# Second batch of an attention kernel: the middle heads' q and k turned by DMA transfers, the first heads' on TensorE behind the last first-layer products

## The chip, the cores and the metric

The kernel runs on one core of one Trainium2 chip. The metric is the device time in microseconds of one execution. Five engines work from queues of their own, each in order: TensorE (PE; its weight loads are listed apart as PEld), VectorE (DVE), ScalarE (ACT), GpSimd (POOL) and SyncE (SP), which here does little but issue DMA transfers. Sixteen DMA engines move the data; in the profile, queue q1 holds what SP issues, q0 what POOL issues.

## The reference, cut to what matters

Eight batches of twelve heads, 448 tokens, 64 columns each; then a two-layer network over the 3584 tokens with 768 columns, 2048 hidden:

```python
q_n, k_n = (rmsnorm(q, g_q), rmsnorm(k, g_k))
scores = scale * np.matmul(q_n, k_n.transpose(0, 1, 3, 2))
attn = softmax(scores)                       # over the keys
x = (attn @ v) -> tokens x (heads * columns)
h = x @ w_in
g = 0.5 * h * (1 + tanh(c * (h + 0.044715 * h**3)))
out = g @ w_out
```

(`softmax` and the arrow stand for the reference's longer lines.)

## The kernel before, in words

The twelve heads of a batch are worked as three groups of four, c = 0, 1, 2: the first, middle and last heads. A group is seven tiles of 64 tokens (t = 0 to 6). For every batch b:

- q and k are loaded by SP (`load`), squared, summed (`total`, L173), and normed (`normed`, L278) into bf16 tiles `nrmq` and `nrmk`, tokens on the partitions.
- They are turned so that the head columns lie on the partitions, into `qT` and `kT`, in one of two ways. `trans` turns on PE: seven transposes for q and seven for k into PSUM (`turn`, L296), each evicted by one instruction (`put`): k always by DVE, which multiplies it with the gains of both norms on the way (L305), q by ACT (L307) or DVE (L309). `transposed` turns by two DMA transposes that SP issues (`dma_trans`, L319), one for q and one for k, straight into `qT` and `kT`; the gains are then multiplied into `kT` in place by DVE (`gain`, L325).
- `unit` (L335) makes the scores of one tile of one group on PE, four products into one PSUM tile pair; `exp` (L343) takes the exponential on ACT. `add_exps` (L355 to L362) sums the exponentials over tiles on DVE, so that PE's sums (`products` with what = 0) need fewer products; `products` with what = 1 gives attn @ v (L387). `turned`, `recip`, `spread` (L397, L402, L409) make the reciprocal of the sums on DVE, and `quad_x` (L422) multiplies it in and writes `xT`.
- The first layer (`mm1_pair`, L556, in batch 0; `mm1_turn`, L537, in batch 1) multiplies `xT` with `win` and puts the GELU into `g` on ACT. The second layer (`quartered`, L495) multiplies `g` with `wout`. It runs interleaved with the attention of the next batch.

That interleaving is an order written out by hand. `SECOND` is the one for b = 1. In its first string, `u` is a unit of scores (the numbering is c = 0, t = 0 to 6, then c = 1, and so on), `8r` are eight rounds of the second layer (four products each), `s` and `x` are the sums and attn @ v of the next group. Its second string is the order of DVE's work: `A0` is the first sum of exponentials of group 0 (L355), `E0` the eviction of a finished second-layer tile (L518), `B0`, `F0`, `G0` the further sums. `L0`, `K0` and the like are hooks: the list `extra` says what is put there, and `first` what DVE gets before the first unit.

Before that, batch 0's first layer runs as f = 0 to 7; after step f the functions that the list `m1` has for f are called. From f = 3 on a step is one pair of products over six weight tiles each, with its GELU (`mm1_pair`). At step 0, DVE and POOL norm the first and last heads of batch 1; at step 2, DVE norms the middle heads (`normed_both(1, 1, nc.vector)`). At step 6 the first heads are turned on PE with q evicted by ACT; at step 7, behind the last pair, the middle heads are turned on PE and evicted by DVE. Under `first`, DVE issues two one-element writes that let SP's loads for batch 2 go (`late_loads`), and then the weight sums `in_sums` (L587 to L589, two groups of three instructions). The last heads of batch 1 are turned by transfers, let go by DVE at `L0` (`late_transposed`), and get their gains at `K0`.

The PSUM tile pairs go round in one list (`rounds`): a unit takes the oldest, and the second layer takes the oldest when its first round is issued.

Of the kernel before, what the change touches and what calls it, by code (L numbers as in the profile page):

```python
# [17 lines left out]
def kernel(  # L18
# [11 lines left out]
    nc = tc.nc  # L30
    B, H, S, D = q.shape
# [86 lines left out]
    def load(b, c, n, parts=1, engs=(nc.sync,)):  # L118
        t = rawqk.tile([P, 2, NT, D], F32, tag=f"raw{n}", name=f"raw{n}")
        src = {"q": q, "k": k}[n]  # L120
        raws[n, b, c] = t
        m = 2 // parts
        return [
            lambda i=i: engs[i].dma_start(
                t[:, i * m:(i + 1) * m].rearrange("p a t d -> p a (t d)"),
                src[b, 4 * c + 2 * i * m:4 * c + 2 * (i + 1) * m].rearrange(
                    "(a r) (p t) d -> (r p) a (t d)", r=2, t=NT
                ),
            )
            for i in range(parts)  # L130
        ]
# [6 lines left out]
    def late_loads(b, c):  # L138

        for n in "qk":  # L140
            for go in load(b, c, n):
                nc.vector.memset(raws[n, b, c][:1, 0, 0, :1], 0.0)
                go()
# [99 lines left out]
    def rsqrt_last(b, c=slice(NCH - 1, NCH)):  # L243

        flat, m = "p c n a t -> p (c n a t)", (c.stop - c.start) * 4 * NT
        y, ms = rinvs[b][:, c].rearrange(flat), sss[b][:, c].rearrange(flat)
        dst, z, u = y, None, ms
        if not steady():
            z, u = oall[0][:, S:S + m], oall[0][:, S + m:S + 2 * m]
            dst = place(b, 1)  # L250
        t = smp.tile([P, NCH * 4 * NT], F32, tag="lg", name="lg")[:, :m]
        nc.vector.tensor_scalar(u, ms, 1.0 / D, 1e-6, op0=ALU.mult, op1=ALU.add)
        nc.vector.tensor_scalar(
            y.bitcast(I32), u.bitcast(I32), -0.5, float(0x5F3759DF), op0=ALU.mult, op1=ALU.add
        )
        for i in range(3):
            if z is not None:
                nc.vector.tensor_copy(z, y)
            half = t if z is None else z
            nc.vector.tensor_mul(t, y if z is None else z, y)  # L260
            nc.vector.scalar_tensor_tensor(half, t, -0.5, u, op0=ALU.mult, op1=ALU.mult)
            nc.vector.scalar_tensor_tensor(
                y if i < 2 else dst, half, 1.5, y, op0=ALU.add, op1=ALU.mult
            )
# [8 lines left out]
    def normed(b, c, n, eng, ts=slice(0, NT)):  # L273
        if (n, b, c) not in nrms:
            nrms[n, b, c] = nrmp.tile([P, NT, 2, D], BF16, tag=f"nrm{n}", name=f"nrm{n}")
        m = ts.stop - ts.start
        root = rinvs[b][:, seat(b, c), "qk".index(n)] if eng is nc.gpsimd else roots[n, b, c]
        eng.tensor_mul(  # L278
            nrms[n, b, c][:, ts].rearrange("p t a d -> p a t d"),
            raws[n, b, c][:, :, ts],  # L280
            root[:, :, ts].to_broadcast([P, 2, m, D]),
        )

    def qT_of(b):
        if b not in qT:
            qT[b] = qkp.tile([128, NCH, NT, 2, R], BF16, tag="qT", name="qT")
        return qT[b]
# [3 lines left out]
    def turn(b, c, n, ts=slice(0, NT)):  # L291

        if ts.start == 0 and ts.stop == NT:
            tps[n] = ps_m.tile([128, 1024], BF16, tag="mm", name="tp")
        for t in range(ts.start, ts.stop):
            nc.tensor.transpose(  # L296
                tps[n][:, t * 128:(t + 1) * 128],
                nrms[n, b, c][:, t].rearrange("p a d -> p (a d)"), ident,
            )

    def put(b, c, n, ts=slice(0, NT), eng=nc.vector):
        dst = (kT if n == "k" else qT_of(b))[:, c, ts]
        src = tps[n][:, :TR].rearrange("p (t r s) -> p t r s", r=2, s=R)[:, ts]
        if n == "k":
            nc.vector.tensor_scalar(dst, src, gcol[:, 0:1], None, op0=ALU.mult)  # L305
        elif eng is nc.scalar:
            nc.scalar.copy(dst, src)  # L307
        else:
            nc.vector.tensor_copy(dst, src)  # L309

    def trans(b, c, eng=nc.vector):
        for n in "qk":
            turn(b, c, n)
            put(b, c, n, eng=eng)

    def dma_trans(b, c, n):

        dst = kT[:, c] if n == "k" else qT_of(b)[:, c]
        nc.sync.dma_start_transpose(  # L319
            dst.rearrange("p t r s -> p t (r s)"),  # L320
            nrms[n, b, c].rearrange("p t a d -> p (t a d)"),
        )

    def gain(b, c):
        nc.vector.tensor_scalar(kT[:, c], kT[:, c], gcol[:, 0:1], None, op0=ALU.mult)  # L325
# [252 lines left out]
    def blocks_of(half, grp):  # L578
        lo, hi = (half * nf // 2 + n for n in BLOCKS[grp])
        return slice(lo * 128, hi * 128)  # L580

    def in_sums(grp):

        f1, f2 = blocks_of(0, grp), blocks_of(1, grp)
        a11, a21, a12, a22 = wv[:, 0, :, f1], wv[:, 0, :, f2], wv[:, 1, :, f1], wv[:, 1, :, f2]
        s2, s3, s4 = wxs[grp]
        nc.vector.tensor_sub(s3, a21, a11)  # L587
        nc.vector.tensor_add(s2, s3, a22)
        nc.vector.tensor_sub(s4, a12, s2)  # L589
# [6 lines left out]
    class Seven:  # L596
# [254 lines left out]
    )  # L851
    SECOND = (
# [441 lines left out]
    def transposed(b, c):  # L1294
        for n in "qk":
            dma_trans(b, c, n)

    def late_transposed(b, c):

        for n in "qk":  # L1300
            dst = kT if n == "k" else qT_of(b)
            nc.vector.memset(dst[:1, c, 0, 0, :1], 0.0)
        transposed(b, c)
# [11 lines left out]
    def normed_both(b, c, eng):  # L1315
        for n in "qk":
            normed(b, c, n, eng)

    for b in range(B):
        m1, side, extra, ends = [], [], [], []  # L1320
        if b == 0:
# [4 lines left out]
                   lambda: normed(1, 0, "k", nc.gpsimd)),  # L1326
                  (2, lambda: total(1, 1, "q"), lambda: total(1, 1, "k"),
                   lambda: normed(1, 0, "q", nc.vector), lambda: rsqrt_last(1),
                   lambda: normed_both(1, 1, nc.vector)),
                  (6, lambda: trans(1, 0, nc.scalar)),  # L1330
                  (7, lambda: trans(1, 1))]
            extra += [("first", lambda: late_loads(2, 0)), ("first", lambda: in_sums("A")), ("first", lambda: in_sums("H")), ("L0", lambda: late_transposed(1, 2)),
                      ("L0", lambda: late_loads(2, 1)), ("a0", lambda: late_loads(2, 2)),
                      ("K0", lambda: gain(1, 2))]

# [147 lines left out]
```

## Time and profile before

| what | value |
|---|---|
| time, median of 3 runs | 381.84 us (381.73 to 381.91) |
| the profiled execution's own time | 381.82 us |
| its span, first to last instruction | 380.0 us |
| PE busy | 371.4 us, 98% |
| DVE busy | 306.3 us, 81% |
| ACT busy | 296.8 us, 78% |
| POOL busy | 140.0 us, 37% |
| mean granted TensorE clock | 0.998 |

The stretch of the change lies between about 46 and 76 us of the span. "Busy" counts instructions, not waits, and an engine with a high share over the whole span need not be the one that sets the pace in a stretch; the chain of waits, followed back from the last instruction, says which it was. A transfer's landing is counted from its issue on the queue.

### The profile page before, as it was taken

What the parts mean: (1) busy time and instruction counts of PE and PEld (TensorE: products, weight loads), DVE (VectorE), ACT (ScalarE), POOL (GpSimd) and SP (SyncE); (2) the same over time, 40 slices, a digit from 0 to 9 for tenths busy, and PEclk for the clock granted to TensorE, in tenths of its full rate; (3) what the DMA queues carried; (4) which work ended last, traced back from release to release, by engine and by line L of the source; (5) the groups of instructions that cost most, each with busy time, mean ns of one, the idle gap of its engine ahead of it and who ended that gap; (6) DMA issues with size and microseconds to landing.
All of it is one profiled execution on the core that took longest, in us unless ns stands there. A gap on an engine that the chain in (4) does not pass through costs nothing.

```text
span 380.0 us, 14862 instructions
## 1 busy us (share of the span) xinstructions
PE 371.4 (98%) x6634; PEld 285.5 (75%) x6634; DVE 306.3 (81%) x469; ACT 296.8 (78%) x383; POOL 140.0 (37%) x127
## 2 busy tenths in 40 slices
PE   8899999999999999999999999999999999999995
PEld 5565577777888977879678876779678786789863
DVE  4999989996899678994799767995699848899863
ACT  6995589767997799976997889977998679966700
POOL 5997503358102780048500781038700560000000
PEclk9999999999999999999999999999999999999999
DMA  7999998799822896258942798139563393320033
GB/s 250 324 240 210 210 245 206 236 160 238 192 54 66 197 242 116 46 115 209 232 104 47 179 203 192 45 86 199 128 111 80 78 121 58 80 57 11 2 73 96
DMA packets 64597, 54.52 MB, mean 143 GB/s; under 512 B 37652, under 2 KB 60436, under 8 KB 64532
## 3 DMA queue, kind: packets, MB, share of 16 engines
q1 hardware_dynamic: 54016, 41.04, 44.2%
q0 software_dynamic: 10128, 11.80, 19.1%
q8 instruction: 52, 0.85, 1.0%
q10 hardware_dynamic: 388, 0.72, 0.5%
q14 instruction: 13, 0.11, 0.1%
HBM read 45.61 MB, written 11.01 MB: 149 GB/s over the span
## 4 chain that ended last, share of the span: by engine, by line
PE 86%; ACT 6%; DVE 4%; DMA 1%; issue 1%; POOL 0%; DVEq 0%
PE t L495 31%; PE t L665 20%; PE t L335 7%; PE t L387 7%; ACT ex L343 5%; PE t L1058 5%; PE t L537 5%; PE t L556 4%; PE t L704 3%; PE t L717 3%; DMA rawq<-in_q_dram 1%; DVE st L397 1%; DVE xT L422 1%; PE h L436 1%; DVE rb L409 1%
## 5 line engine op out<-in xcount | busy, mean ns | idle before, releaser
L343 ACT ACTIVATE ex<-t,shift 128x896 bf16<-128x896 f32 x168 | 157.1, 1012 | 4.2 <-PE t L335 3.4
L495 PE MATMUL t<-wout,g 64*64 64x384 bf16 (+1 forms) x3456 | 150.0, 305 | 0.0
L495 PEld LDWEIGHTS <-g 64*64 64x64 bf16 x3456 | 103.5, 107 | 29.3 <-issue 2.0
L335 PE MATMUL t<-qT,kT 64*64 64x448 bf16 x672 | 57.0, 351 | 1.4 <-ACT ex L343 0.6
L173 DVE TENSOR_REDUCE ss<-sq 128x14 f32<-128x896 f32 (+3 forms) x50 | 44.4, 911 | 9.9 <-ACT sq L162 5.2
L1186 POOL COPY mark<-es 1x1 bf16<-1x1 bf16 x7 | 1.2, 177 | 127.6 <-DVE es L362 118.5
L665 PEld LDWEIGHTS <-win 128*128 128x128 bf16 x456 | 43.7, 98 | 3.5 <-issue 2.1
L278 POOL TENSOR_TENSOR nrmq<-rawq,rinv 128x896 bf16<-128x896 f32 (+1 forms) x21 | 34.8, 1659 | 19.0 <-ACT rinv L205 10.7
L278 POOL TENSOR_TENSOR nrmk<-rawk,rinv 128x896 bf16<-128x896 f32 (+1 forms) x21 | 34.4, 1640 | 0.0
L387 PE MATMUL t<-ex,vb 64*64 64x448 bf16 x588 | 31.9, 350 | 0.0
L335 PEld LDWEIGHTS <-kT 64*64 64x64 bf16 x672 | 23.4, 106 | 9.3 <-DVE kT L305 1.2
L387 PEld LDWEIGHTS <-vb 64*64 64x64 bf16 x672 | 23.3, 107 | 7.5 <-issue 0.9
L689 ACT ACTIVATE g<-t 128x896 bf16<-128x896 f32 (+1 forms) x36 | 26.1, 758 | 3.6 <-DVE t L683 3.6
L397 DVE STREAM_TRANSPOSE st<-t 128x448 f32<-128x448 f32 x42 | 24.8, 628 | 5.0 <-PE t L387 2.9
L355 DVE TENSOR_TENSOR es<-ex 128x1792 bf16<-128x1792 bf16 x21 | 22.3, 1063 | 7.5 <-ACT ex L343 7.5
L409 DVE STREAM_TRANSPOSE rb<-rc 128x896 f32<-128x896 f32 (+1 forms) x25 | 26.7, 1067 | 0.3
L665 PE MATMUL t<-xs,win 128*128 128x224 bf16 x228 | 24.9, 259 | 0.0
L665 PE MATMUL t<-xT,win 128*128 128x224 bf16 x228 | 24.6, 259 | 0.3
L513 ACT COPY osb<-t 128x768 f32<-128x768 f32 (+1 forms) x18 | 12.6, 702 | 14.0 <-PE t L495 14.0
L422 DVE TENSOR_TENSOR xT<-t,rb 128x896 bf16<-128x896 f32 x21 | 22.8, 1086 | 0.9
L164 POOL TENSOR_TENSOR sq<-rawk 128x896 f32<-128x896 f32 (+1 forms) x14 | 21.9, 1569 | 1.1 <-DMA rawk<-in_k_dram 1.1
L358 DVE TENSOR_TENSOR es<-es,ex 128x1792 bf16<-128x1792 bf16 x21 | 22.3, 1063 | 0.0
(167 smaller groups left out, 574.9 us busy)
## 6 DMA issues: line engine op xcount, KB each, us to landing
rawq<-in_q_dram SPq DMA_DIRECT2D x22, 448.0 KB, 4.4
rawk<-in_k_dram SPq DMA_DIRECT2D x22, 448.0 KB, 5.4
out_dram<-osb SPq DMA_DIRECT2D x38, 192.0 KB, 2.9
vb<-in_v_dram POOLq DMA_DIRECT2D x6, 672.0 KB, 7.2
win<-in_moe_w_in_dram POOLq DMA_DIRECT2D x8, 384.0 KB, 11.4
out_dram<-osb SPq DMA_DIRECT2D x31, 96.0 KB, 2.6
wout<-in_moe_w_out_dram POOLq DMA_DIRECT2D x3, 768.0 KB, 17.8
vb<-in_v_dram POOLq DMA_DIRECT2D x2, 448.0 KB, 15.8
```

What stands on the lines that cost most here:

```text
L173: nc.vector.reduce_sum(sss[b][:, seat(b, c), "qk".index(n), hs, ts], squares(b, c, n, hs, ts), axis=AX.X)
L278: eng.tensor_mul(nrms[n, b, c][:, ts].rearrange("p t a d -> p a t d"), raws[n, b, c][:, :, ts], root[:, :, ts].to_broadcast([P, 2, m, D]),)
L335: nc.tensor.matmul(sc[r * R:(r + 1) * R, a, :S], kT[rs, c, t, r], qT[b][rs, c, :, r], start=True, stop=True,)
L343: nc.scalar.activation(exs[b, c][:, t], scs.pop((b, c, t))[:, :, :S], AF.Exp, scale=scale, bias=shift)
L355: nc.vector.tensor_add(es, ex[:, :2], ex[:, 2:4])
L387: nc.tensor.matmul(o[r][a * D:(a + 1) * D], vb[min(b, 1)][rs, 2 * c + a, i] if what else ones[rs], es[i][rs, a], start=(i == 0), stop=(i = ...
L397: nc.vector.transpose(st[:, r].rearrange("p a b -> p (a b)"), o[r])
L409: nc.vector.transpose(oas["rb"][:, rs].rearrange("p r s -> p (r s)"), rc.to_broadcast([128, (rs.stop - rs.start) * m, 32]),)
L422: nc.vector.tensor_mul(xT[b][:, 2 * c:2 * c + 2], oas["o", c, 1][:, :, :S], oas["rb"])
L495: mm = nc.tensor.matmul(o[a * R:(a + 1) * R, bank, :hi - lo], g[rs, f, at:at + R], wout[rs, f, lo:hi], start=(n == 0), stop=(n == len(step ...
L665: nc.tensor.matmul(t[:, bank, n * QS:(n + 1) * QS], lhs[:, m, n * 128:(n + 1) * 128], self.rhs[i][:, m], start=i == owner and n == m == 0, ...
L689: nc.scalar.activation(g[:, f:f + m, lo:lo + QS], (self.of(name) if src is None else src).rearrange("p r (n s) -> p r n s", n=2), AF.Gelu_ ...
```

## The change

For batch 1 only. The middle heads (c = 1) are no longer turned on PE: at step 2, straight after they are normed, SP issues the two DMA transposes, and their gains are multiplied in place by DVE at the end of the work under `first`. The first heads (c = 0) are turned on PE at step 7 and no longer at step 6, and q is evicted by DVE and no longer by ACT. The written order begins with six rounds of the second layer, then the first unit, then three rounds, where it began with the first unit and eight rounds; up to the fourth unit the number of rounds is the same as before (17).

```diff
     SECOND = (
-        "u 8r uu 9r u 7r uu 10r u 3r u 5r u 2r u 4r us 6r u 3r u 1r u 6r xu 4r u 5r u 1r u"
+        "6r u 3r uu 8r u 7r uu 10r u 3r u 5r u 2r u 4r us 6r u 3r u 1r u 6r xu 4r u 5r u 1r u"
         " 3r s 1r u 2r u 10r u 2r x 1r s 3r x",
...
                    lambda: normed(1, 0, "q", nc.vector), lambda: rsqrt_last(1),
-                   lambda: normed_both(1, 1, nc.vector)),
-                  (6, lambda: trans(1, 0, nc.scalar)),
-                  (7, lambda: trans(1, 1))]
-            extra += [("first", lambda: late_loads(2, 0)), ("first", lambda: in_sums("A")), ("first", lambda: in_sums("H")), ("L0", lambda: late_transposed(1, 2)),
+                   lambda: normed_both(1, 1, nc.vector), lambda: transposed(1, 1)),
+                  (7, lambda: trans(1, 0))]
+            extra += [("first", lambda: late_loads(2, 0)), ("first", lambda: in_sums("A")), ("first", lambda: in_sums("H")), ("first", lambda: gain(1, 1)), ("L0", lambda: late_transposed(1, 2)),
                       ("L0", lambda: late_loads(2, 1)), ("a0", lambda: late_loads(2, 2)),
                       ("K0", lambda: gain(1, 2))]
```

VectorE's queue from the end of the norming of the middle heads to the first work at `L0`, before (`tp` is a PSUM tile of turned q or k, `wx` and `vb_121` the homes of the weight sums, `es` a sum of exponentials):

```order
L305 TENSOR_SCALAR kT<-tp,gcols 128x896
L309 COPY qT<-tp 128x896
L305 TENSOR_SCALAR kT<-tp,gcols 128x896
L142 MEMSET rawq 1x1
L142 MEMSET rawk 1x1
L587 TENSOR_TENSOR wx<-win 128x1536
L588 TENSOR_TENSOR wx<-wx,win 128x1536
L589 TENSOR_TENSOR wx<-win,wx 128x1536
L587 TENSOR_TENSOR vb_121<-win 128x768
L588 TENSOR_TENSOR vb_121<-vb_121,win 128x768
L589 TENSOR_TENSOR vb_121<-win,vb_121 128x768
L355 TENSOR_TENSOR es<-ex 128x1792
```

and now:

```order
L309 COPY qT<-tp 128x896
L305 TENSOR_SCALAR kT<-tp,gcols 128x896
L142 MEMSET rawq 1x1
L142 MEMSET rawk 1x1
L587 TENSOR_TENSOR wx<-win 128x1536
L588 TENSOR_TENSOR wx<-wx,win 128x1536
L589 TENSOR_TENSOR wx<-win,wx 128x1536
L587 TENSOR_TENSOR vb_121<-win 128x768
L588 TENSOR_TENSOR vb_121<-vb_121,win 128x768
L589 TENSOR_TENSOR vb_121<-win,vb_121 128x768
L325 TENSOR_SCALAR kT<-kT,gcols 128x896
L355 TENSOR_TENSOR es<-ex 128x1792
```

Of three evictions two are left, now both of the first heads, and the gains of the middle heads (L325) stand between the weight sums and the first sum of exponentials.

SP's queue of DMA issues at the same place, as a difference; the two loads behind the new rows are those of batch 2 that DVE lets go under `first`:

```order
 L124 DMA rawq<-in_q_dram 128x2x448
 L124 DMA rawk<-in_k_dram 128x2x448
+L319 DMA_TRANSPOSE qT<-nrmq 128x7x128
+L319 DMA_TRANSPOSE kT<-nrmk 128x7x128
 L124 DMA rawq<-in_q_dram 128x2x448
 L124 DMA rawk<-in_k_dram 128x2x448
```

The two new transposes go out ahead of those loads; nothing else on this queue has moved.

## The prediction

> **What bounds the kernel now.** I read the page first, then the chain of waits around the place that the change touches, then VectorE's timeline there, then the DMA queues in stretches.
>
> ```profile
> span 380.0 us, 14862 instructions
> PE 86%; ACT 6%; DVE 4%; DMA 1%; issue 1%; POOL 0%; DVEq 0%
> ```
>
> TensorE (PE) sets the end nearly everywhere, so a microsecond taken from its queue is worth one if nothing else is late. The profiled execution took 381.82 us, 1.82 more than its span; the median is 381.84, so sums against either agree. In the chain of waits (start, length, what) the stretch from the last products of the first layer to those of the second batch reads:
>
> ```profile
> 47.39 2.27 PE t L556 x12
> 49.66 0.78 PE tp L296 x14
> 50.44 0.31 PE t L335 x4
> ...
> 54.19 1.14 PE t L495 x28
> ...
> 57.52 0.49 PE t L495 x12
> 58.01 0.19 PE t L335 x4
> ...
> 67.49 3.71 ACT ex L343 x4
> ...
> 71.25 1.08 DVE es L358
> ...
> 75.30 1.19 DVE st L397 x2
> ...
> 76.53 3.56 PE t L537 x69
> ```
>
> Fourteen transposes (0.78) stand on PE's path before the first scores. PE holds the path to 67.5, ScalarE's (ACT) exponentials to 71.2, VectorE (DVE) to 76.5, and then PE's first-layer products wait for DVE's last reading of a PSUM tile. Three engines are therefore close together here. DVE's timeline (start, length, line, what, wait before it):
>
> ```profile
> 47.28 1.08 DVE L278 TENSOR_TENSOR nrmk<-rawk,o 128x896 bf16<-128x896 f32 x1
> 48.27 0.68 DVE L305 TENSOR_SCALAR kT<-tp,gcols 128x896 bf16<-128x896 bf16 x1
> 50.09 0.62 DVE L309 COPY qT<-tp 128x896 bf16<-128x896 bf16 x1 [1.14 <-PE tp L296]
> 50.63 0.68 DVE L305 TENSOR_SCALAR kT<-tp,gcols 128x896 bf16<-128x896 bf16 x1
> 51.24 0.95 DVE L587 TENSOR_TENSOR wx<-win 128x1536 bf16<-128x1536 bf16 x1
> ...
> 55.74 1.08 DVE L355 TENSOR_TENSOR es<-ex 128x1792 bf16<-128x1792 bf16 x1
> ...
> 57.05 1.02 DVE L518 COPY osb<-t 128x384 f32<-128x384 f32 x2 [0.17 <-PE t L495]
> ...
> 61.03 1.18 DVE L397 STREAM_TRANSPOSE st<-t 128x448 f32<-128x448 f32 x2 [0.56 <-PE t L387]
> ...
> 64.54 0.40 DVE L325 TENSOR_SCALAR kT<-kT,gcols 128x896 bf16<-128x896 bf16 x1
> ```
>
> From 51.24 DVE runs without a gap into L355, the first sum of exponentials. After 55.74 it waits twice, 0.17 and 0.56; the 0.56 is the way from its own last sum (L362) through PE's sums back to L397, so it moves with DVE and is no reserve. The table by stretches (PE, weight loads, DVE, ACT, POOL) shows what follows:
>
> ```profile
> 61.00:76.50 15.50, 15.40 (x352) 11.11 (x345) 15.18 (x24) 13.26 (x19) 6.37 (x7) 1.00 0.79 238
> ```
>
> DVE is busy 15.18 of 15.50 us. What it is late at 61 it is late at 76.5, and PE behind it.
>
> **The change part by part.** *Removed from PE:* the 14 transposes of the middle heads, 0.78 us. Those of the first heads move behind the last pair of products, 14 as before. *ACT* loses one eviction ahead of its last GELU, where it waited for PE anyway.
>
> ```profile
> 50.63 1.28 ACT L1438 ACT_TABLE_LOAD   x1
> 51.92 13.00 ACT L343 ACTIVATE ex<-t,shift 128x896 bf16<-128x896 f32 x14
> ```
>
> The last products end 0.78 earlier, and so do the GELU, the table load, and the first exponential (51.92 to 51.14). The transposes of the first heads then run from 48.9 to 49.7; DVE evicts q and k by its two rows above, 0.78 earlier: 49.31 and 49.85 to 50.53. Six rounds of second-layer products (24 products; 28 took 1.14, so 0.98) lead PE to 50.6 before the first scores, which therefore wait for nothing. That exposed wait I cost at 0; without the six rounds it would be about 0.9. The rounds are only moved. On DVE one eviction from PSUM (0.68) becomes one scaling in SBUF (L325, 0.40), and the weight sums begin at 50.5 and end at 55.05.
>
> *Added:* two DMA transposes and a wait. SP issues them as soon as DVE has made q (47.4) and k (48.4); its queue is empty then. The wait is DVE's L325 for k's landing. Queued behind it on DVE is L355 and everything above after 55.05; behind that on PE are the scores of the middle heads (the L335 piece at 58.01 is their first), and the sums that feed L397. So the change hangs on when k lands. DMA issues on SP (start, length), and landings (us after issue, last number) of the loads and transposes nearest in time, asked for by the stretch of their issue:
>
> ```profile
> 51.39 0.37 SPq L124 DMA_DIRECT2D rawq<-in_q_dram  x1
> ...
> 57.02 1.33 SPq L319 DMA_TRANSPOSE qT<-nrmq  x1
> 58.46 1.24 SPq L319 DMA_TRANSPOSE kT<-nrmk  x1
> ```
>
> ```profile
> rawq<-in_q_dram SPq DMA_DIRECT2D x1, 448.0 KB, 6.6
> qT<-nrmq SPq DMA_TRANSPOSE x1, 3.4
> kT<-nrmk SPq DMA_TRANSPOSE x1, 3.0
> vb<-in_v_dram POOLq DMA_DIRECT2D x1, 448.0 KB, 21.5
> ```
>
> By the 3.0 of 58.46 k would land at 52 and be hidden under the weight sums. But these transposes ran when the engines were free. Packets by queue (packets, MB, share) of four stretches, 52.7 to 54, 50.5 to 58, 55 to 58, and 58.2 to 60.9:
>
> ```profile
> q0 software_dynamic: 298, 0.27, 125.5%
> ```
>
> ```profile
> q0 software_dynamic: 948, 0.89, 72.2%
> ```
>
> ```profile
> q0 software_dynamic: 60, 0.05, 10.1%
> ```
>
> ```profile
> q1 hardware_dynamic: 1870, 0.49, 101.6%
> ```
>
> POOL's queue q0 (the second layer's weights, then v) fills all 16 engines until about 55. From 52.7 to 54 SP's queue q1 moves nothing at all, though a load was issued on it at 51.39; that load lands at 51.39 + 6.6 = 57.99. Earlier, from 22 to 25.5, with both queues full, they went one packet for one:
>
> ```profile
> q0 software_dynamic: 248, 0.47, 71.2%
> q1 hardware_dynamic: 247, 0.44, 38.0%
> ```
>
> The two transposes are some 1,800 small packets (1,870 in the 2.7 us in which both ran, a few of a load among them). Whether q1 waits for q0 or alternates with it, the 948 packets of q0 give out before the second transpose does, so k ends behind q0. *Earliest*: q0's bulk ends at 55.0, q has shared until then, k alone takes 1.35 (half of 2.7), and landing lags by 0.6 (61.46 against 60.9): 57.0. *Latest*: one engine carries q0 to the last (60 packets after 55; the v load issued at 36.95 lands at 58.45), all of both follows: 58.45 + 2.7 = 61.1. *Taken*: the transposes stand on q1 ahead of the load that landed at 57.99, so q gets its place, and k comes 1.0 later (60.42 to 61.46 is the spacing of the two that ran free): 59.0. Then L325 to 59.4, and L355 starts at 59.4 instead of 55.74: +3.66, of which the 0.17 wait is absorbed: **+3.5**. PE's 0.78 and ACT's 0.78 are lost in it, because both then wait for DVE. The stalled middle scores alone would cost less (59.4 against 58.0). Sum: 381.82 + 3.5 = **385.3**; with 57.0 and 61.1 it is 383.3 and 387.4.
>
> [...] The row 58.2 to 60.9 shows 0.49 MB in 2.7 us, about 180 GB/s, with a load among it; the measurement decides. [...]
>
> **The rivals.** *Hidden after all* (not slower): k lands by 55.05. For it: the weight sums cover 4.6 us, and the free transposes took 3.0. Against it: no q1 packet in 52.7 to 54. L325 then ends at 55.45, L355 gains 0.29, the 0.17 goes: 381.82 − 0.46 = 381.4. Only if DVE's full stretch gives way too does PE's whole 0.78 come through: 381.0. From a landing 0.5 us later, at 55.5, it is a loss.
>
> *Long turns*: SP's transposes pass in long bursts between q0's packets, and it is the weights that come late. POOL's last weight load and the landings of the last two:
>
> ```profile
> 33.44 0.73 POOL L1176 DMA_DIRECT2D wout<-in_moe_w_out_dram  x1
> ...
> wout<-in_moe_w_out_dram POOLq DMA_DIRECT2D x2, 384.0 KB, 19.5
> ```
>
> The last lands near 53.4 (a median of two: the first, issued 0.7 earlier, lands a little sooner); PE needs it in the piece at 54.19, about 54.8, after the change 54.0. Pushed back by all of 2.7 us it comes at 56.1, PE stands 2.1, and 381.82 − 0.78 + 2.1 = 383.1, with k in time. Against it: one for one at 22 to 25.5. [...]
>
> That the transfers don't start early, so that the change doesn't do what it says, gets no chance of its own: nothing unfinished stands ahead of them on SP, whose next issue before was at 51.39.
>
> **How the numbers follow.** Forecast 0.72, spanning 383.3 to 387.4; long turns 0.06; hidden 0.16; hidden with PE's gain whole 0.05; later still than 61.1, 0.01. No change is within 0.2% (0.76 us), about what a measurement here can tell: faster 0.05 (381.0), same 0.16 (381.4), slower 0.79. The range reaches to the hidden case, 381.3 to 387.0; the likeliest case's own is 383.3 to 387.0.
>
> **What would show it.** Right: DVE's L325 after the weight sums waits 2 to 6 us on a DMA; the first transpose lands near 58, the second near 59; L355 starts near 59.4; PE's middle scores wait for kT; PE's first L537 comes near 79. The head start shows too: first exponential near 51.1. Wrong: L325 starts at once at 55; or the stall at L325 is there and DVE makes it up before L537; or PE waits for the weights near 54.

## The result, and the profile after

The changed kernel takes 386.80 us (median of 6 executions, 385.57 to 388.67) against 381.94 for the kernel before (6, 381.73 to 383.64): a ratio of 1.0129, 95% interval 1.0108 to 1.0149. It is slower by some 4.9 us; its profiled execution took 385.96, with a span of 384.2 (before: 381.82 and 380.0). Medians are of all executions; the ratios leave out those more than 1.5% above the fastest of the same kernel, which are two of ten for no_wait and one of ten for k_alone.

The chain of waits of the changed kernel, from the end of the first layer to the second batch's products (start, length, what):

```profile
37.45 11.17 PE t L556 x60
48.63 10.44 DMA kT<-nrmk
...
59.46 1.08 DVE es L355
...
79.54 1.19 DVE st L397 x2
...
80.77 3.37 PE t L537 x65
```

The DMA that turns k now stands on the path, with 10.44 us from issue to landing. On the path the products of L537 begin at 80.77 instead of 76.53. VectorE's timeline shows the wait in its place:

```profile
49.77 0.68 DVE L305 TENSOR_SCALAR kT<-tp,gcols 128x896 bf16<-128x896 bf16 x1
...
54.41 0.56 DVE L589 TENSOR_TENSOR vb<-win,vb 128x768 bf16<-128x768 bf16 x1
59.09 0.45 DVE L325 TENSOR_SCALAR kT<-kT,gcols 128x896 bf16<-128x896 bf16 x1 [4.12 <-DMA kT<-nrmk]
59.46 1.08 DVE L355 TENSOR_TENSOR es<-ex 128x1792 bf16<-128x1792 bf16 x1
...
63.32 0.62 DVE L362 TENSOR_TENSOR es<-es,ex 128x896 bf16<-128x896 bf16 x1
65.26 1.18 DVE L397 STREAM_TRANSPOSE st<-t 128x448 f32<-128x448 f32 x2 [1.31 <-PE t L387]
```

The weight sums end at 54.97, and VectorE then stands 4.12 us for k. L397 waits 1.31 where it waited 0.56 before. The two new issues on SP's queue:

```profile
47.19 1.33 SPq L319 DMA_TRANSPOSE qT<-nrmq  x1
48.63 4.50 SPq L319 DMA_TRANSPOSE kT<-nrmk  x1
53.23 0.52 SPq L124 DMA_DIRECT2D rawq<-in_q_dram  x1
```

The second issue holds SP for 4.50 us, so the load behind it leaves at 53.23 instead of 51.39. From 47 to 51, with the first transpose issued at 47.19, POOL's queue q0 moves 582 packets and q1 none at all; q1's first packet comes 3.9 us behind that issue, between 51.05 and 51.10. From then on they share: from 54.0 to 54.5 the two queues move (packets, MB, share):

```profile
q0 software_dynamic: 84, 0.07, 89.4%
q1 hardware_dynamic: 84, 0.02, 32.2%
```

Over this stretch they get one packet for one. A transposed packet here carries 0.25 KB (0.02 MB in 84), a packet of q0 about 0.8 KB, so the transposes get few of the bytes that move. The late first packet and the sharing together made a landing of 10.44 us out of one of 3.0; how much each of them took was not separated.

TensorE's middle scores wait for the gain, and one piece later again:

```profile
59.60 0.38 PE L335 MATMUL t<-qT,kT 64*64 64x448 bf16 x4 [2.27 <-DVE kT L325]
...
61.61 0.59 PE L335 MATMUL t<-qT,kT 64*64 64x448 bf16 x4 [0.82 <-DVE osb L518]
...
64.61 0.53 PE L387 MATMUL t<-es,ones 64*64 64x448 bf16 x4
```

TensorE then gets a lower clock. The table by stretches (stretch, its length, then PE, weight loads, VectorE, ScalarE and POOL, each with its count; the three last numbers are granted clock, DMA share, GB/s):

```profile
60.00:62.00 2.00, 1.18 (x28) 0.68 (x24) 2.00 (x8) 1.01 (x1) 0.00 (x0) 0.87 0.49 163
62.00:64.00 2.00, 2.00 (x32) 1.40 (x28) 1.81 (x3) 1.75 (x2) 0.00 (x0) 0.50 1.16 186
64.00:66.00 2.00, 2.00 (x44) 1.49 (x40) 0.74 (x2) 1.27 (x2) 1.99 (x3) 0.77 0.81 127
```

From 62 to 64 TensorE is busy throughout at half the clock and makes 32 products; from 66 to 68, at 1.00, it makes 56. VectorE's last sum (L362) ends at 63.94, but TensorE's queue comes to the sums' products (the L387 piece) only at 64.61. This is why L397 waits longer than before.

### The profile page after: what moved, and what is told of

Read it like the earlier page. It is cut to its first block, busy times and chain, and to the rows that moved or that the text cites. A ratio compares the mean times of both kernels' runs of the same rounds, so it can differ in the third digit from the quotient of the medians.

```text
span 384.2 us, 14839 instructions
## 1 busy us (share of the span) xinstructions
PE 371.4 (97%) x6620; PEld 284.7 (74%) x6620; DVE 305.6 (80%) x469; ACT 296.9 (77%) x382; POOL 140.2 (36%) x127
## 3 DMA queue, kind: packets, MB, share of 16 engines
q1 hardware_dynamic: 55872, 41.50, 44.6%
## 4 chain that ended last, share of the span: by engine, by line
PE 83%; ACT 6%; DVE 5%; DMA 4%; issue 1%; POOL 0%; DVEq 0%
PE t L495 29%; PE t L665 20%; PE t L387 7%; PE t L335 7%; ACT ex L343 5%; PE t L1058 5%; PE t L537 5%; PE t L556 4%; PE t L704 3%; PE t L717 3%; DMA kT<-nrmk 3%; DMA rawq<-in_q_dram 1%; DVE st L397 1%; DVE xT L422 1%; PE h L436 1%
## 5 line engine op out<-in xcount | busy, mean ns | idle before, releaser
L495 PE MATMUL t<-wout,g 64*64 64x384 bf16 (+1 forms) x3456 | 152.3, 306 | 0.1
L335 PE MATMUL t<-qT,kT 64*64 64x448 bf16 x672 | 58.7, 355 | 4.5 <-DVE kT L325 2.3
L335 PEld LDWEIGHTS <-kT 64*64 64x64 bf16 x672 | 24.2, 107 | 13.2 <-DVE kT L325 2.6
L387 PE MATMUL t<-ex,vb 64*64 64x448 bf16 x588 | 32.0, 350 | 0.0
L397 DVE STREAM_TRANSPOSE st<-t 128x448 f32<-128x448 f32 x42 | 24.8, 629 | 6.1 <-PE t L387 4.0
L387 PEld LDWEIGHTS <-vb 64*64 64x64 bf16 x672 | 23.7, 107 | 7.3 <-issue 1.0
L355 DVE TENSOR_TENSOR es<-ex 128x1792 bf16<-128x1792 bf16 x21 | 22.3, 1061 | 7.1 <-ACT ex L343 7.1
```

Source lines behind the costliest of these rows:

```text
L335: nc.tensor.matmul(sc[r * R:(r + 1) * R, a, :S], kT[rs, c, t, r], qT[b][rs, c, :, r], start=True, stop=True,)
L355: nc.vector.tensor_add(es, ex[:, :2], ex[:, 2:4])
L387: nc.tensor.matmul(o[r][a * D:(a + 1) * D], vb[min(b, 1)][rs, 2 * c + a, i] if what else ones[rs], es[i][rs, a], start=(i == 0), stop=(i = ...
L397: nc.vector.transpose(st[:, r].rearrange("p a b -> p (a b)"), o[r])
L495: mm = nc.tensor.matmul(o[a * R:(a + 1) * R, bank, :hi - lo], g[rs, f, at:at + R], wout[rs, f, lo:hi], start=(n == 0), stop=(n == len(step ...
```

## The experiments

Thirteen timelines are compared by one ruler. VectorE makes 24 reciprocals (L402, one for each of the 8 batches' 3 groups). For each kernel the start of such an instruction less its start in the kernel before (20.19, 62.24, 71.02, 120.78, 150.20, 340.33 us) says how late the program is there; the same difference at the first one, which lies ahead of anything changed and is between −0.24 and +1.15, is taken off. L402 and its neighbours move by one or two lines where a kernel has lines added.

| kernel | batch 1, first (62.24) | batch 1, second (71.02) | batch 2, third (120.78) | batch 3, first (150.20) | last (340.33) | median time, us |
|---|---|---|---|---|---|---|
| the change | 4.32 | 4.31 | 4.32 | 4.69 | 4.69 | 386.80 |
| again | 4.03 | 4.02 | 4.13 | 4.82 | 4.77 | 386.17 (one) |
| v_after_gain | 0.41 | 3.67 | 3.69 | 3.69 | 4.18 | 386.19 |
| v_after_sums | 1.45 | 1.44 | 1.77 | 2.72 | 3.02 | 383.30 |
| before_v_after_sums | 0.29 | 0.29 | 0.29 | 0.30 | 0.33 | 381.92 |
| gain_late | 3.95 | 3.97 | 4.02 | 4.40 | 4.37 | 386.27 |
| fillers | 4.15 | 4.15 | 4.15 | 4.15 | 4.16 | 385.78 |
| both_late | 0.18 | 1.09 | 1.07 | 1.07 | 1.08 | 384.13 |
| no_wait | −0.61 | 2.17 | 2.16 | 2.16 | 2.17 | 384.37 |
| nw_again | −0.60 | 1.68 | 2.09 | 2.72 | 3.30 | 384.65 (one) |
| k_alone | −0.61 | 0.54 | 0.53 | 0.53 | 1.11 | 382.62 |
| no_transfers | −0.61 | −0.61 | −0.61 | 0.08 | 2.03 | 383.27 |
| nt_again | −0.61 | −0.61 | −0.60 | 0.06 | 0.04 | 381.78 (one) |

The first column's reciprocal serves the first heads; its sums are made while the middle heads are scored. The kernel before gave medians of 381.9 to 382.1 in every comparison.

### The change once more

The changed kernel, unaltered, for a second trace.

> The changed kernel a second time, unaltered, for a second profile: its six times lie 3 us apart (385.6 to 388.7), and the one profile cannot say where. Theory: k's transpose lands behind POOL's queue at 57 to 61 us, VectorE's L325 waits for it, PE stands idle and then gets about half the clock for some microseconds; a later landing or a longer half clock gives the longer times. Expected: L325 starts 58 to 61, first L397 of the stretch 64.5 to 68, and all of the difference to the first profile lies before the first products of batch 1's first layer (L537, 80.8 there). Rival: the spread arises later in the program, and L537 starts at 80.8 again whatever the time is.

It took 386.17 us. VectorE:

```profile
59.66 0.45 DVE L325 TENSOR_SCALAR kT<-kT,gcols 128x896 bf16<-128x896 bf16 x1 [4.59 <-DMA kT<-nrmk]
...
65.09 1.18 DVE L397 STREAM_TRANSPOSE st<-t 128x448 f32<-128x448 f32 x2 [0.57 <-PE t L387]
```

The wait comes back at 4.59 us. The clock fell here too (0.64 from 60 to 62, 0.51 from 62 to 64), and yet L397 waits 0.57 as before: k was 0.57 later, and the sums were no later. So the fall of the clock need not cost anything. The expectation that all of the difference to the first profile lies ahead of L537 missed: at the second reciprocal this trace is 0.29 less late than the first profile, and from batch 3 on 0.1 later.

### What k shares the engines with: v moved behind k

In the changed kernel POOL issues batch 1's v in two loads near 37 us, behind the weights. Here it issues v in one load when the middle heads' gain is done.

```diff
-  ..., lambda: load_v(1, 0, 2), lambda: load_v(1, 2, 4)),
...
   ("first", lambda: gain(1, 1)),
+  ("first", lambda: gpsimd_waits(kT[:1, 1, 0, 0, :1])), ("first", lambda: load_v(1, 0, HP)),
```

> Batch 1's v is loaded in one transfer that POOL issues only when the middle heads' gains are multiplied in, so that POOL's queue holds nothing but the second layer's weights when the transposes go. Theory (k waits its turn behind and among POOL's packets): k lands by 54.5 to 55.5, L325 follows the weight sums at once or within 0.5 us, no stretch of PE below 0.9 of the clock, time 381.4 (381.0 to 381.9). Rival (the transposes are slow by themselves when issued at 47, since the second one held SP for 4.5 us): k still lands at 57 or later and the time stays above 383.5. If v then comes too late for attn @ v (63 us), PE waits there instead and the time is 383 to 385 although L325 doesn't wait.

It took 386.19 us (385.86 to 388.63), ratio 1.0126 (1.0092 to 1.0159). VectorE's two gains of the batch, the middle heads' and the last heads':

```profile
56.13 0.45 DVE L325 TENSOR_SCALAR kT<-kT,gcols 128x896 bf16<-128x896 bf16 x1 [0.97 <-DMA kT<-nrmk]
...
68.33 0.45 DVE L325 TENSOR_SCALAR kT<-kT,gcols 128x896 bf16<-128x896 bf16 x1 [3.19 <-DMA kT<-nrmk]
```

The middle k lands 3 us sooner, the wait shrinks from 4.12 to 0.97, and the batch is only 0.41 late there. It still lands 7.3 us after its issue, and later than the 54.5 to 55.5 expected. But v, issued at 57.57, now runs against the last heads' transposes (issued 57.68 and 59.53), and their gain, which waited for nothing before, waits 3.19. TensorE first waits 1.53 for v itself, up to 66.14, as the expectation's last sentence had it, and then 1.19 for that gain, up to 68.84. The crowd has moved one group on and costs nearly the same.

### v between the two, and the same in the kernel before

v goes after the first weight sum (issued 53.60).

```diff
   ("first", lambda: in_sums("A")),
+  ("first", lambda: gpsimd_waits(wx[:1, 2, 0, :1])), ("first", lambda: load_v(1, 0, HP)),
   ("first", lambda: in_sums("H")),
```

> As the kernel before in this call, but v is let go earlier, when the first group of VectorE's weight sums is done (about 53.3 us), so that it lands with time to spare. Theory: as there, 381.4 (381.0 to 381.9), v lands by 61. Rival (transposes slow by themselves): above 383.5. A third way: v's packets at 55 still meet the second transpose, k lands near 56, and the time is 382.3.

> The kernel before with only this later load of v (when the first group of weight sums is done): the control, which separates what the later load does by itself from what it does for the transposes. Theory: nothing waits for v before 63 us, so 381.8 as before (381.5 to 382.1). Rival: the late load of v is a gain or a loss of its own of over 0.5 us, by what it frees or crowds among the loads of batch 2.

With the change 383.30 us (381.95 to 384.57), ratio 1.0030 (1.0010 to 1.0051); in the kernel before 381.92, ratio 1.0003 (0.9993 to 1.0014). So v's place alone costs nothing, and v in front of k is worth 3 us to the change (4.32 against 1.45 at the first reciprocal). The time lies 1 us above the third way's 382.3 and under the rival's 383.5; 381.4 was missed. What is left, VectorE and then TensorE:

```profile
56.81 0.45 DVE L325 TENSOR_SCALAR kT<-kT,gcols 128x896 bf16<-128x896 bf16 x1 [2.01 <-DMA kT<-nrmk]
```

```profile
55.30 0.52 PE L495 MATMUL t<-wout,g 64*64 64x384 bf16 x8 [1.14 <-DMA wout<-in_moe_w_out_dram]
```

VectorE still waits 2.01 for k, although POOL's queue moves only 49 packets from 52 to 55; what holds k there was not found. And now TensorE waits 1.14 for the weights. From 50 to 52 this kernel's queues moved

```profile
q1 hardware_dynamic: 372, 0.10, 104.7%
q0 software_dynamic: 175, 0.25, 68.2%
```

two packets of the transposes for one of the weights. The one for one of the changed kernel is no rule, and the wait that the rival with the late weights describes is there in this kernel.

### Which queue pays for the wait: the gain moved behind the sums

```diff
-  ("first", lambda: gain(1, 1)),
+  ("J0", lambda: gain(1, 1)),
```

> The changed kernel with the middle heads' gain moved on VectorE's queue from ahead of the first sum of exponentials to behind the last one (L362) of the first heads. Theory, VectorE's queue behind the wait is what the wait costs: the first sum of exponentials starts near 55.1 instead of 59.46, VectorE gets to the gain near 59.5 to 60 and k has landed by then (59.1), TensorE's middle scores start near 60.2, VectorE's L397 comes near 63.5 instead of 65.3, and the time is about 384.3 us (383.5 to 385.2). Rival, TensorE's standing still ahead of the middle scores sets the cost by itself: then the time stays within 0.5 us of the changed kernel's 386.2 to 386.8. The fall of the clock after TensorE's stand stays in both.

386.27 us (385.91 to 386.96), ratio 1.0095 (1.0065 to 1.0126): the rival's number, and the expected 384.3 fell. VectorE now does its five sums and evictions first, and the gain without a wait:

```profile
60.92 0.45 DVE L325 TENSOR_SCALAR kT<-kT,gcols 128x896 bf16<-128x896 bf16 x1
66.12 1.18 DVE L397 STREAM_TRANSPOSE st<-t 128x448 f32<-128x448 f32 x2 [4.76 <-PE t L387]
```

(This trace runs 1.15 later from the start.) TensorE:

```profile
61.42 0.38 PE L335 MATMUL t<-qT,kT 64*64 64x448 bf16 x4 [2.88 <-DVE kT L325]
```

VectorE is free from 61.4 and waits 4.76 us for TensorE, whose first middle scores start at 61.42 and whose sums for L397 stand behind four pieces of middle scores, three of them at a lower clock (0.63 from 62 to 64, 0.52 from 64 to 66). So VectorE's queue is not the only one that carries the delay: TensorE's order alone does it. The clock falls here after a single stand of 2.88 us.

### The clock: work for TensorE during the wait

```diff
 def unit(b, c, t):
+    if (b, c, t) == (1, 1, 0):
+        idle(12, sc[:, 0])
```

(the tile is the unit's own, which its scores then overwrite).

> The changed kernel with twelve products of a constant tile put ahead of the middle heads' first scores on TensorE's queue (about 2.2 us of work whose result nobody reads), so that TensorE works during most of the wait for k. Theory, the clock of one half after the stand is what made the delay 4.2 and not 3.5 us: k still lands near 59 and the gain runs then, but the granted clock stays at 1.00 between 61 and 65, the middle scores take 0.39 us apiece, VectorE's first L397 waits 0.56 instead of 1.31, and the time is 0.7 us under the changed kernel's (385.5 against 386.2 for a like run). Rival, the clock falls for another reason or the later pieces do not matter: no difference over 0.3 us, or the clock still falls.

385.78 us (385.44 to 387.26), ratio 1.0088 (1.0053 to 1.0122). VectorE, and the stretch in which the changed kernel had half the clock:

```profile
59.73 0.45 DVE L325 TENSOR_SCALAR kT<-kT,gcols 128x896 bf16<-128x896 bf16 x1 [4.71 <-DMA kT<-nrmk]
...
65.15 1.18 DVE L399 STREAM_TRANSPOSE st<-t 128x448 f32<-128x448 f32 x2 [0.56 <-PE t L389]
```

```profile
62.00:64.00 2.00, 1.74 (x36) 1.15 (x35) 1.86 (x4) 1.32 (x2) 0.00 (x0) 1.00 0.87 141
```

The clock stays at 1.00 and L397 waits 0.56, as the theory had it. The stand ahead of the middle scores is down to 0.44; the later one of 0.82 is still there. That the fall came from TensorE standing is shown; that it costs 0.7 us is not, since "again" had both the fall and the short wait, and the intervals of the two kernels overlap.

### Both cures together

v after the first weight sum, and the gain behind the first sum of exponentials (hook `L0`).

> The kernel that lets v go late (after the first weight sum) and has the middle heads' gain behind the first sum of exponentials instead of ahead of it. Theory: k lands at 56.4 as in the kernel with the late v alone, the first sum of exponentials starts near 55.1 and covers the wait but for 0.7 us, the first L397 comes at 61.6 to 61.9 (62.23 with the late v alone, 61.03 before), and the 1.1 us that TensorE waits for wout stays: 382.3 to 383.0 us, not under the kernel before. Rival, VectorE's wait was all that was left of the loss: 381.4 us or less, faster than before.

384.13 us (381.73 to 385.54), ratio 1.0045 (1.0020 to 1.0070); the profiled execution took 382.81.

```profile
56.52 0.45 DVE L325 TENSOR_SCALAR kT<-kT,gcols 128x896 bf16<-128x896 bf16 x1 [0.54 <-DMA kT<-nrmk]
...
61.15 1.18 DVE L397 STREAM_TRANSPOSE st<-t 128x448 f32<-128x448 f32 x2 [0.56 <-PE t L387]
```

The wait for the middle k is down to 0.54 and the batch 0.18 late, better than the 0.6 to 0.9 expected. The last heads are 1.09 late all the same, and the time is not under that of the kernel before; the median is even above the 383.0 that was expected at most, and the one trace, of a shorter execution, does not show why. The rival, in which VectorE's wait was all that was left, fell.

### Nobody waits for k

```diff
 def unit(b, c, t):
+    w = 0 if (b, c) == (1, 1) else c
...
-        ..., kT[rs, c, t, r], qT[b][rs, c, :, r],
+        ..., kT[rs, w, t, r], qT[b][rs, w, :, r],
...
-  ("first", lambda: gain(1, 1)),
+  ("first", lambda: nc.vector.tensor_scalar(nrms["k", 1, 0], nrms["k", 1, 0], gcol[:, 0:1], ...)),
```

> The changed kernel with its two new transposes still sent, but nobody waits for them: the middle heads' scores are made from the first heads' turned q and k, and VectorE's gain (L325 in the changed kernel) works on a normed tile of k that is there (so the middle heads' attention is wrong, all the work stays). Theory, the wait for k is the whole loss: the gain starts without a wait near 55.0 and ends at 55.4, the first sum of exponentials starts near 55.5 (before: 55.74), the second reading of the sums (the x2 piece before 76.5) ends 0.2 to 0.5 earlier than before, the clock stays 1.00 from 56 to 68, and the time is 381.4 us, between 380.9 and 382.0. Rival, the transfers cost elsewhere (they hold back the second layer's weights, or the moved transposes and rounds cost): TensorE waits about 1 us for wout near 55, or the loss shows elsewhere, and the time is 382.5 us or more.

The middle heads' own scores are left out here. 384.37 us (382.48 to 389.14), ratio 1.0052 (1.0023 to 1.0080). The theory that the wait is the whole loss fell. Its first half holds: VectorE

```profile
55.47 1.08 DVE L356 TENSOR_TENSOR es<-ex 128x1792 bf16<-128x1792 bf16 x1
...
60.57 1.18 DVE L398 STREAM_TRANSPOSE st<-t 128x448 f32<-128x448 f32 x2 [0.56 <-PE t L388]
```

is 0.61 ahead at the first reciprocal. At the next one it is 2.17 late. In between, TensorE stands, and waits for nothing that the profile shows:

```profile
63.37 0.32 PE L496 MATMUL t<-wout,g 64*64 64x384 bf16 x1 [1.95 <-issue]
```

The profile finds no semaphore that this product or the weight load behind it waited for. What came 2.47 us ahead of its resuming is a packet on q8, the queue that the profile calls instruction, which starts within the 0.05 us from 60.90 (packets, MB, share; the share is of 0.05 us, so 1.386 x 16 x 0.05 = 1.1 us of one engine):

```profile
q8 instruction: 1, 0.02, 138.6%
```

q8 moves 52 such packets in an execution. And the last heads' transposes, issued at 56.64 and 59.00 behind the new ones and the held-up loads, land after

```profile
qT<-nrmq SPq DMA_TRANSPOSE x1, 7.7
kT<-nrmk SPq DMA_TRANSPOSE x1, 6.2
```

us, where they took 3.4 and 3.0 before. A second trace was taken of it.

> The kernel in which nobody waits for the turned k, with both transfers sent, once more unaltered, for a second trace. Theory, the packets hold up TensorE's instruction blocks every time: first L398 0.4 to 0.7 us earlier than before, then TensorE stands without any semaphore between 59 and 64 by 1 us or more, again resuming 2.3 to 2.5 us after a q8 block's start, and the second half of the batch is 1 to 3 us late. Rival, the 1.95 us was chance: no such stand, and the gain of 0.5 us lasts to 121 us.

384.65 us. The gain of 0.60 comes back, and so does a delay in the second half (1.68), but by another road: TensorE's stand without a semaphore is 0.15 us only, so the expectation of 1 us or more missed. VectorE:

```profile
63.79 1.09 DVE L173 TENSOR_REDUCE ss<-sq 128x14 f32<-128x896 f32 x1 [1.83 <-POOL sq L164]
...
66.22 0.45 DVE L325 TENSOR_SCALAR kT<-kT,gcols 128x896 bf16<-128x896 bf16 x1 [0.32 <-DMA kT<-nrmk]
```

POOL's square had waited 1.98 for batch 2's q, whose load had left SP at 53.78, behind the second transpose's issue (4.98 us), and landed 8.2 us later; VectorE's reduction waits for POOL, and the last heads' gain, behind it, still finds k late (the last transposes took 7.5 and 7.6 us). TensorE then waits for that gain:

```profile
66.72 0.38 PE L336 MATMUL t<-qT,kT 64*64 64x448 bf16 x4 [1.48 <-DVE kT L325]
```

### The dose: no transfer, one, two

The same kernel without the two new transposes, and with k's alone (`dma_trans(1, 1, "k")` in the place of `transposed(1, 1)`).

```diff
-  lambda: normed_both(1, 1, nc.vector), lambda: transposed(1, 1)),
+  lambda: normed_both(1, 1, nc.vector)),
```

> As the kernel in which nobody waits for the middle heads' turned k, and the two new transposes are not sent at all (the middle heads' attention stays wrong, all other work is there). Theory, the transposes' packets themselves cost some 2 us besides the wait, by holding up what else travels on the DMA engines, the blocks of TensorE's own instructions (queue q8) above all: without them TensorE's stand of 1.95 us near 61 to 63, in which it waited for no semaphore, is gone, the blocks on q8 start 5.5 to 7 us apart as before, the second reading of the sums behind the last heads ends 0.2 to 0.5 us earlier than before, and the time is 381.0 to 381.6 us with a spread like that of the kernel before. Rival, the stand comes from the new order (the first heads' transposes moved, six rounds first): it stays, and the time stays at 383 to 385 us.

> As the kernel in which nobody waits for the middle heads' turned k, but only k is turned by a transfer and q is not sent (same wrong attention of the middle heads). Theory, it is the amount of small packets that counts: about 930 new ones instead of 1,860, the queue is empty of them 1.3 to 2 us sooner, the time lies between the kernel without the transfers (about 381.3) and the one with both (384.4), near 382.5 us. Rival, any transfer there costs the same, or what costs is that SP's queue is held by the second transpose's issue: 384 us with one as with two, or as little as with none.

In batch 1 (second column of the table) none gives −0.61, one +0.54, two +2.17 and +1.68. The last heads' own transposes land after

```profile
qT<-nrmq SPq DMA_TRANSPOSE x1, 3.9
kT<-nrmk SPq DMA_TRANSPOSE x1, 3.1
```

with none, and

```profile
qT<-nrmq SPq DMA_TRANSPOSE x1, 5.5
kT<-nrmk SPq DMA_TRANSPOSE x1, 4.9
```

with one. So sending the two transposes (1,856 small packets: q1 carries 55,872 with them, 54,016 without) costs by itself, whether or not anyone waits for what they bring; the new order and the moved transposes of the first heads cost batch 1 nothing. With k alone SP's issue took 1.34 us and not 4.89, and the time was 382.62 (382.13 to 383.47, and one execution of 991.34; interval of the ratio 1.0006 to 1.0031), as expected. One transfer costs 1.15 without holding SP: batch 2's first load leaves at 50.61, as it does with none (50.55). With two it leaves at 53.82 and 53.78. So the second transfer's cost can come from its packets or from the held issue, as the second rival says, and in nw_again that late load is on the way to the delay; the runs do not separate the two.

The time without the transfers, 383.27 (382.47 to 385.15; ratio 1.0041, 1.0023 to 1.0059), is not the 381.0 to 381.6 that was expected: the gain of batch 1 is there and is lost later. TensorE near batch 3's first sums, and VectorE's gain in the last batch:

```profile
148.20 0.51 PE L496 MATMUL t<-wout,g 64*64 64x384 bf16 x6 [0.35 <-issue]
```

```profile
317.43 0.45 DVE L325 TENSOR_SCALAR kT<-kT,gcols 128x896 bf16<-128x896 bf16 x1 [3.08 <-DMA kT<-nrmk]
```

The kernel before has no stand at the first place, and a wait of 1.09 at the second. A second trace of it:

> The kernel without the transfers once more, unaltered, for a second trace. Its 383.3 us lie 1.4 above the kernel before although batch 1 gained 0.66 in the first trace; that trace lost 0.69 near 148 us (TensorE stood without a wait) and 2.0 near 317 us (VectorE waited 3.08 us for a transposed k of the last batch, 1.1 before). Theory, both come from the new distance between TensorE's progress and the transfers and come back: a stand near 148 of 0.3 to 1.0 us, a wait near 317 of 2 us or more, 382.5 to 384.5 us. Rival, they are chance of one execution: one of them or both are missing, the time may still be the same for another reason.

381.78 us (the kernel before beside it: 382.08).

```profile
148.13 0.51 PE L496 MATMUL t<-wout,g 64*64 64x384 bf16 x6 [0.34 <-issue]
```

```profile
315.22 0.45 DVE L325 TENSOR_SCALAR kT<-kT,gcols 128x896 bf16<-128x896 bf16 x1 [0.95 <-DMA kT<-nrmk]
```

The stand near 148 is there again and takes the whole gain back (0.66); the long wait near 317 is not, so not every execution has it. The 382.5 us or more that were expected did not come either. Six of the other kernels' traces (the change, again, v_after_sums, gain_late, nw_again and this one's first) have a stand at the very same place (in the change and gain_late it shows on the weight load alone, 0.41 each), and six have none.

## Why the prediction was right, point by point

- **The head start.** First exponential 51.14, measured 51.07; the evictions 49.31 and 49.85, measured 49.23 and 49.77; weight sums ended 55.05, measured 54.97; the first scores waited for nothing behind the six rounds. Right.
- **Where and how long VectorE waits.** Landing of q near 58, measured 58.29 (47.19 + 11.1); of k 59.0, within 57.0 to 61.1: measured 59.07, 59.64 and 59.71 (the gains' starts, less 0.02; the change, again, fillers). L355 at 59.4: measured 59.46, 60.03 and 60.09. Right; v_after_gain and v_after_sums show that v's packets are part of the cause, since k comes 2.3 to 3 us sooner when v is behind them. The rest, against 3.0 us on free engines, stays open.
- **Sharing.** "Whether q1 waits for q0 or alternates with it": it did both, no packet for 3.9 us, then one for one (343 and 343 from 53.5 to 55.5), but not as the rule it was taken for (two to one in v_after_sums). Equal counts over a stretch give the share of each queue and not the length of a turn, so neither they nor the rows at 22 to 25.5 speak against long turns. The late weights of that rival did not come in the changed kernel; a wait of TensorE for them, 1.14 us in v_after_sums and 0.59 in both_late, does.
- **The sum, +3.5.** The mechanism was right and the sum too small: L537 came 4.24 late, not 3.5. The mis-sized term is "the 0.56 is the way from its own last sum through PE's sums back to L397, so it moves with DVE": in the profiled execution it grew to 1.31, because TensorE's queue, behind by the stalled scores and for a time at half the clock, came to the sums 0.67 after VectorE was done, and that 0.75 is the difference. In "again" it did not grow; there k was 0.57 later instead. "PE's first L537 comes near 79" did not even fit the text's own sum (76.53 + 3.5 = 80.0). The profiled execution, 385.96, is 4.14 above the one before; of the later delays only the stand in batch 3 (0.37 here, 0.69 in "again") is located. The median, 386.80, is 0.8 above the profiled execution, and no trace shows where that lies. It falls inside the range by luck: the part above 385.3 was there for a k that lands later than 59.0, up to 61.1, which is not what filled it in the profiled execution.
- **"The stalled middle scores alone would cost less".** It put 1.4 on them (59.4 against 58.0). With VectorE's queue free of the wait, TensorE's order alone gave 3.95. The gain came at 60.92 there, which is 59.77 less that trace's 1.15, some 0.6 later than in the changed kernel (59.17 with its 0.08 taken off), so at k's landing it would be some 3.3 (an estimate, 3.95 less 0.6): far above 1.4.
- **"PE's 0.78 and ACT's 0.78 are lost in it".** Right, and they would be lost otherwise too: without transfers batch 1 ends 0.61 ahead (the rival's own working had 0.46), and TensorE's stand in batch 3 takes 0.69 and 0.66 back.
- **"Hidden after all", 381.4.** The step that failed is in this rival: it priced a k in time as if the transfers were then free. no_wait had k's wait gone, did what the rival said as far as the first L397, and took 384.4. Sending the two transfers delays what follows (the last heads' transposes, the loads, in no_wait TensorE's own stand of 1.95) and costs 2.3 to 2.8 us in batch 1 by itself (1.68 and 2.17 against −0.61). In the changed kernel the stall pushes the last heads' transposes back to 60.63, when the engines are free again (they land after 3.4 and 2.9 us); the second reciprocal is no later than the first (4.31 and 4.32), and the sum for the change did not need this term. The ways to "faster" did.

What stays open: why k still takes 7.3 to 8.4 us to land with v out of its way; whether the second transfer costs by its packets or by holding SP; why TensorE stands at one instruction of batch 3 in seven of the thirteen traces and not in the others; and why the kernel without transfers took 383.3 in one comparison and 381.8 in a single later execution.

## What to carry to other kernels

Before a transfer replaces work on an engine, look at what the queues carry between its issue and the first reader, and at what is issued behind it until the queues are free again: a transfer's landing on free engines (3.0 us) says nothing of its landing in a crowd (10.4), and sending it can delay its neighbours even when nobody waits for what it brings (in no_wait the last heads' transposes landed after 7.7 and 6.2 us, before after 3.4 and 3.0). Put the first reader behind other work on its queue only after asking which engine waits for it in turn; and a gain of half a microsecond in one stage is to be followed to the end of the program before it is believed.

## What the runs showed of the hardware that was not expected

- **A second transpose holds its issuer under load.** Its issue took SP 4.50 us (4.89 and 4.98 in the kernels in which nobody waits, 2.47 with v out of the way in v_after_gain) against 1.24 with free engines and 1.34 when it was the only one under load.
- **TensorE stands without a wait, 2.4 us behind a q8 packet.** In nine of ten stands of TensorE without a semaphore, found in nine of the traces, it resumed 2.3 to 2.5 us after the start of a q8 packet (63.37 against 60.90, 148.20 against 145.80, in the change the weight load's 152.78 against 150.44, and so on), in the tenth, the first of nw_again, 2.66; three smaller ones, of 0.23 to 0.28 us (both_late, no_wait, k_alone), ended 2.3 to 2.5 behind one too. The lag is shown. q8's packets go with TensorE's work: in the kernel before the two that start at 191.38 and 194.77 have 172 products and weight loads between them, the two at 32.27 and 50.33, five times as far apart, 230. That TensorE waits in these stands for what q8 brings, and that a crowded DMA engine makes these packets late, is the author's estimate from that and from the dose (near 61 to 63 no stand without transfers, 0.32 with one, 1.95 and 0.15 with two); the runs do not settle it.
- **Half a clock after a stand.** After a stand of 2.27 us (the change), 2.71 (again) or 2.88 (gain_late) TensorE got 0.50 for some 3 us; it came within 0.4 us of work in "again" and after 1.1 us in gain_late, with no second stand before it. With filler products, which cut the stand to 0.44, it kept 1.00, and so it did after stands of 1.95 (no_wait) and of 1.53 and 1.19 (v_after_gain). From what length of stand on the clock falls, these runs do not show.
